# Pooled attention and a gated MLP on one core: fewer VectorE steps for scales, unread TensorE products, a new written order

## Chip, cores and metric

The kernel runs on one core of a Trainium2 chip, in one launch. The metric is the device time of one execution in microseconds (us), the median of several runs. Five engines work side by side, each with its own queue in order: TensorE (PE, with its weight loads as PEld), VectorE (DVE), ScalarE (ACT), GpSimd (POOL) and SyncE (SP), which here only issues DMAs: loads, stores and transposes.

## The reference

```python
# q, k, v: (8, 8, 576, 64); pool 8; float64 weights w_in (512, 1024), w_out (1024, 512), g_ln (1024)
k_p = k.reshape(B, H, 72, 8, D).mean(axis=3)
v_p = v.reshape(B, H, 72, 8, D).mean(axis=3)
scores = scale * q @ k_p.T
attn = softmax(scores)                      # with 1e-9 in the denominator
x = (attn @ v_p), rows as (batch, position), columns as (head, d): (4608, 512)
h = x @ w_in
solu = h * softmax(h)                       # over 1024 columns
ln = (solu - mean) / sqrt(var + 1e-6) * g_ln
out = ln @ w_out                            # (4608, 512) float32
```

The weights arrive as float64, in pairs of 32-bit words, and the results are wanted close to float32. The kernel therefore splits every factor of a large product into two float16 parts, high and low, after scaling it by a power of two, and sums three products (high by high, high by low, low by high).

## The kernel before, in words

*Tiles.* The 4608 rows are worked in 36 tiles of 128 rows. A pair of batches makes nine tiles: four of the first, a mixed one (64 rows of each, key `("m", g)`), four of the second. For a tile i: `q_hi` and `q_lo` split q, `q_T` turns it by a DMA transpose (tile 0 on TensorE: `q_Tp`, `q_Tc`), `scores` multiplies with the pooled and turned k, `s_max`, `s_sub`, `s_exp`, `e_sum`, `e_rec`, `e_mul` are the softmax (one PSUM buffer, so `scores` of a tile waits for `e_mul` of the one before), `e_hi`, `e_lo`, `e_T` split and turn the result, `av` multiplies with pooled v, `x_hi` and `x_lo` make the split input of the MLP. `mm1` (three parts, 48 products of 512 columns in all, two at a time on the halves of the array) gives h in PSUM; `h_max`, `h_nb`, `h_exp`, `z_scale`, `z_mul` are the gated softmax, `z_cen`, `z_hi`, `z_lo`, `z_var` the normalization and split, `z_T` two DMA transposes, `mm2` (three parts, 48 products) the output, `n_u`, `n_f` its row factor on POOL, `o_evac` and `o_store` scale and store it.

*Weights.* Eight chunks of 1 MB are loaded (`w_load`), four for each matrix. For each, ScalarE takes a rough value and the sign (`w_exp`, `w_sgn`), VectorE shifts and joins the words into a float32 (`w_shift`, `w_tail`), POOL puts the sign on (`w_mul`), TensorE sums the rough values into a bound for the largest magnitude (`w_bnd`). From the bound a scale, a power of two, is made (`w_rmax`, `w_par`, `w_all`, then `wi_scale` or `wo_scale`), and the chunks are split: `w_hi` on ScalarE, the low part by `w_res` on TensorE (product with a scaled identity, less the high part) and `w_lo` on ScalarE, or by `w_lod` on VectorE. `g_T`, `g_put`, `g_max`, `g_par`, `g_all` do the same for the gain g.

*k and v of a batch.* They are loaded in three pieces (`load_kv`); for batch 0 the rows are pooled on TensorE by products with the identity (`pool_pe`, copied by `pool_ev`), for the others on POOL (`pool_kv`). `a_max` takes each partition's largest magnitude, `a_par` spreads it to all partitions by a product (`spread`), `a_all` reduces, and three VectorE steps `a_scale` make the power of two "p" and its reciprocal "s": floor and factor 2^-14, keeping the exponent bits (`exp_bits`), reciprocal. `h_bat` (POOL) multiplies v's scale with the three factors `pw3` that `wi_scale` leaves; `h_nb`, `h_exp` and `z_scale` of the batch's tiles read that.

*Order.* Nothing is scheduled at run time but by semaphores. The table `ORDER` gives every operation a position in one list; each engine works its own operations in that order and waits where an input or a buffer isn't ready. Where this text says that one operation stands ahead of another, it means this table. Buffers: seven for raw loads, in PSUM one for scores, one for attention products and spreads, two for h (shared with pooling, residues and TensorE's transposes), one for outputs.

*Lines.* Most products are recorded at the helper `mm`, line 272; `pool_pe` 405, `k_Tp` 513, `w_bnd` 650, `w_res` 809 and 812, `q_Tp`/`e_Tp` 882, `av` 998; on VectorE `a_max` 425, `q_max` 437, `a_all` 487, `a_scale` 492, 275 and 499, `w_shift` 638, `wi_scale` 706 to 713, `v_lo` 578, `q_lo` 865, `e_mul` 948, `h_max` 1040; on ScalarE `w_exp` 634, `e_Tc` 899, `o_evac` 1150; on POOL `w_mul` 678, `h_bat` 721. In the rows kr, vr are raw k and v, kp, vp pooled, amx the magnitudes, gk, gv spread, pk, sk the scale, hp is h, op the output in PSUM, wir, wor raw weights, u_ their rough values.

## Time and profile before

| | us |
|---|---|
| median of 3 runs (lowest, highest) | 493.37 (492.62, 495.02) |
| the profiled execution | 493.96 |
| its span, first to last instruction | 492.2 |
| TensorE busy | 464.2 (94%) |
| VectorE busy | 371.7 (76%) |
| ScalarE busy | 332.2 (67%) |
| POOL busy | 305.8 (62%) |
| mean granted clock of TensorE | 0.996 |

The span is what the trace covers; the execution's time is 1.8 us longer. Busy shares are averages over stages of different kinds: loading and splitting the weights together with batch 0 at first, then a long even stretch of tiles, then the last tiles. [...]

### The profile page before, as it was taken

The numbers are of one execution on the slowest core, as the hardware profiler recorded it, in microseconds if no ns is written. First come the engines' busy times: TensorE is split into PE (matmuls) and PEld (weight loads), VectorE is DVE, ScalarE is ACT, GpSimd is POOL, SyncE is SP. The second block draws the span as 40 slices with busy tenths as digits, with TensorE's granted clock in tenths as the row PEclk, the third lists the DMA queues.
The fourth block names the chain that finished last, engine by engine and source line by source line (L and its number), as shares of the span: only waits on it lengthen the run. The fifth ranks groups of instructions, "written<-read, shape, count | busy, mean of one in ns | idle before, by whom it ended". The sixth has DMA issues, their size and how long they took to land.

```text
span 492.2 us, 14712 instructions
## 1 busy us (share of the span) xinstructions
PE 464.2 (94%) x5976; PEld 301.0 (61%) x5976; DVE 371.7 (76%) x808; ACT 332.2 (67%) x521; POOL 305.8 (62%) x520
## 2 busy tenths in 40 slices
PE   3698699999999999999999999999999999999996
PEld 3574355565667667766755555555566666666663
DVE  3898899997888878897859887788778769553320
ACT  4577997857867687767549656766766767674551
POOL 1556654896668686956792687554986437618340
PEclk9999899999999999999999999999999999999999
DMA  8998668997999996997979979998999485647252
GB/s 301 359 309 197 160 103 188 182 215 165 216 213 216 201 217 128 247 178 209 189 174 166 179 200 204 188 143 174 212 215 171 114 156 125 116 102 136 55 117 87
DMA packets 197940, 88.92 MB, mean 181 GB/s; under 512 B 174312, under 2 KB 182512, under 8 KB 197360
## 3 DMA queue, kind: packets, MB, share of 16 engines
q1 hardware_dynamic: 197872, 87.98, 85.8%
q8 instruction: 47, 0.77, 0.7%
q14 instruction: 21, 0.17, 0.1%
HBM read 36.70 MB, written 9.44 MB: 94 GB/s over the span
## 4 chain that ended last, share of the span: by engine, by line
PE 63%; DVE 10%; POOL 10%; DMA 7%; ACT 4%; issue 3%; SPq 2%; POOLq 0%; ACTq 0%; DVEq 0%
PE op L272 27%; PE hp L272 26%; PE xp L998 4%; PE sc L272 3%; POOL vr L395 2%; DMA wir<-in_moe_w_in_dram 2%; DMA zT<-z 2%; DMA vr<-in_v_dram 2%; POOL kr L395 2%; POOL z L1092 2%; PE vrps L405 1%; DVE z L1072 1%; DVE m L1040 1%; POOL kp L395 1%; PE res_wo L809 1%
## 5 line engine op out<-in xcount | busy, mean ns | idle before, releaser
L272 PE MATMUL hp<-wi,xT 128*64 128x512 f16 x1728 | 197.7, 379 | 1.0 <-ACT xT L1007 0.9
L272 PE MATMUL op<-wo,zT 128*64 128x512 f16 x1728 | 197.7, 379 | 0.8 <-DMA zT<-z 0.6
L272 PEld LDWEIGHTS <-xT 128*64 128x64 f16 x1728 | 110.2, 110 | 70.4 <-ACT xT L1007 1.4
L272 PEld LDWEIGHTS <-zT 128*64 128x64 f16 x1728 | 111.3, 110 | 67.0 <-DMA zT<-z 1.1
L1092 POOL TENSOR_TENSOR z<-z,z 128x512 f16<-128x512 f32 x71 | 82.8, 1175 | 56.9 <-ACT z L1086 55.5
L1040 DVE TENSOR_REDUCE m<-hp 128x1 f32<-128x1024 f32 x36 | 43.9, 1218 | 27.1 <-PE hp L272 25.1
L977 POOL TENSOR_TENSOR e<-e,e 128x512 f16<-128x512 f32 x36 | 42.6, 1184 | 31.4 <-ACT e L969 31.3
L1051 ACT ACTIVATE z<-hp,nb,Hb 128x1024 f32<-128x1024 f32 x32 | 38.3, 1198 | 20.3 <-DVE nb L1043 18.4
L1072 DVE SCALAR_TENSOR_TENSOR z<-hp,rs,z 128x1024 f32<-128x1024 f32 x36 | 46.1, 1279 | 5.9 <-ACT z L1051 4.8
L1081 ACT ACTIVATE z<-z,sz 128x1024 f32<-128x1024 f32 x36 | 41.1, 1143 | 13.3 <-DVE z L1072 13.3
L1150 ACT ACTIVATE osb<-op,f 128x512 f32<-128x512 f32 x36 | 24.5, 680 | 29.5 <-PE op L272 23.9
L395 POOL TENSOR_TENSOR kr<-kr 128x512 f32<-128x512 f32 (+3 forms) x42 | 36.9, 886 | 9.3 <-DMA kr<-in_k_dram 8.6
L395 POOL TENSOR_TENSOR vr<-vr 128x512 f32<-128x512 f32 (+3 forms) x42 | 36.7, 878 | 5.7 <-DMA vr<-in_v_dram 3.7
L1086 ACT ACTIVATE z<-z 128x1024 f16<-128x1024 f32 x36 | 37.9, 1052 | 2.0 <-issue 1.4
L933 DVE TENSOR_REDUCE sc<-sc 128x8 f32<-128x576 f32 x36 | 27.4, 761 | 14.9 <-ACT sc L929 14.9
L1105 ACT ACTIVATE junk<-z 128x1024 f16<-128x1024 f32 x36 | 37.7, 1048 | 0.2
L919 DVE TENSOR_REDUCE mx<-sc 128x8 f32<-128x576 f32 x36 | 27.0, 750 | 10.7 <-PE sc L272 10.7
L998 PEld LDWEIGHTS <-vb 128*64 128x64 f16 x960 | 29.1, 111 | 7.0 <-DMA eT<-e 1.3
L998 PE MATMUL xp<-eT,vb 128*64 128x128 f16 (+1 forms) x960 | 31.1, 215 | 1.2 <-DMA eT<-e 0.9
L272 PEld LDWEIGHTS <-qT 128*64 128x64 f16 x1152 | 25.0, 114 | 9.0 <-issue 5.1
L272 PE MATMUL sc<-kT,qT 128*64 128x72 f16 x1152 | 25.9, 200 | 3.8 <-DVE e L948 2.7
L1011 DVE SCALAR_TENSOR_TENSOR xT<-xp,xT 128x512 f16<-128x512 f32 x36 | 24.6, 683 | 5.7 <-ACT xT L1007 5.5
(239 smaller groups left out, 625.8 us busy)
## 6 DMA issues: line engine op xcount, KB each, us to landing
kr<-in_k_dram SPq DMA_DIRECT2D x16, 512.0 KB, 5.3
qr<-in_q_dram SPq DMA_DIRECT2D x16, 512.0 KB, 5.8
vr<-in_v_dram SPq DMA_DIRECT2D x32, 256.0 KB, 5.4
out_dram<-osb SPq DMA_DIRECT2D x32, 256.0 KB, 4.3
wor<-in_moe_w_out_dram SPq DMA_DIRECT2D x4, 1024.0 KB
wo<-in_moe_w_in_dram SPq DMA_DIRECT2D x2, 1024.0 KB
wir<-in_moe_w_in_dram SPq DMA_DIRECT2D x2, 1024.0 KB, 10.9
zT<-z SPq DMA_TRANSPOSE x72, 3.9
```

The source lines that it names most:

```text
L272: nc.tensor.matmul(out[lo : lo + 64] if m > 64 else out, lhsT=lhsT[:, lo : lo + 64], **kw)
L395: nc.gpsimd.tensor_tensor(out=dst, in0=src[:, :, :n], in1=src[:, :, n : 2 * n], op=ALU.add)
L933: nc.vector.tensor_reduce(out=tl[i]["r0"], in_=s_view(i), axis=AX.X, op=ALU.add)
L977: nc.gpsimd.tensor_tensor(out=e_main(i, 1), in0=e_src(i)[0], in1=e_main(i, 0), op=ALU.subtract)
L998: nc.tensor.matmul(xp[64 * e : 64 * e + 64, c, lo:hi], lhsT=vb[b % 2][:, n, c, e], rhs=eT[:, 2 * c + e if n < 2 else H + c // 2, lo:hi], s ...
L1040: nc.vector.tensor_reduce(out=small(i, "m"), in_=tl[i]["hp"], axis=AX.XY, op=ALU.max)
L1051: nc.scalar.activation(z, t["hp"], AF.Exp, bias=t["nb"], scale=hsc(i, 0), accum_out=small(i, "se"))
L1072: nc.vector.scalar_tensor_tensor(out=t["z"], in0=t["hp"], scalar=t["rs"], in1=t["z"], op0=ALU.mult, op1=ALU.mult, accum_out=small(i, "sz"),)
L1081: nc.scalar.activation(t["zf"], t["zf"], AF.Identity, bias=t["sz"], scale=-float(DFF))
L1086: nc.scalar.activation(t["z16"][:, 0], t["zf"], AF.Copy)
L1092: eng.tensor_tensor(out=t["z16"][:, 1, fs], in0=t["zf"][:, fs], in1=t["z16"][:, 0, fs], op=ALU.subtract)
L1105: nc.scalar.activation(junk, t["zf"], AF.Square, scale=DFF**-0.5, accum_out=small(i, "V"))
```

## The change

Four things. First, steps of scales on VectorE: the factor 2^-14 of the k and v scales is put into the bfloat16 identity `identb` that spreads the maxima, and the floor into a bit that `exp_bits` now sets, so `a_scale` (three steps) becomes `a_unit` (two). `wi_scale` goes from seven steps to three on VectorE, the three factors becoming one POOL product (`w_pwi`, with constants `c3`). `wo_scale` goes from eight steps to five, two more stand in `g_all`, and one product goes to POOL (`w_pwo`). Second, `idle` issues products of a constant matrix with itself into a corner of a PSUM buffer that nothing reads, ahead of the real products of that buffer, in eleven places and 167 in all. Third, dependencies: `h_bat` waits for `pw3` from POOL, `n_f` for `pwo` from POOL. Fourth, `ORDER` is a new table throughout.

In the new table, by queues. SP's loads begin with two chunks of w_in, the last piece of k of batch 0, the third chunk, half of q, and then k's first and second piece (before: k's first piece, two chunks, k's last piece, the third chunk, k's second piece, q). v of batch 0 is loaded around the second chunk of w_out, ahead of the third and fourth (before: its second piece behind the fourth). TensorE: the bounds of the first three chunks ahead of the large pieces of k; `k_Tp` directly behind `q_Tp`; all of v of batch 0 pooled ahead of the first residue of w_in; `v_rep` of batch 0 behind `scores` of tile 3 (before: ahead). Up to `mm1` of tile 0 the same operations as before. VectorE: ahead of `e_mul` of tile 2 no longer one `q_max` of batch 1, one `v_lo` of batch 0 and `a_all` of k of batch 1. ScalarE: `r_put` ahead of `e_Tc`; `x_hi` of tile 0 ahead of a part of `e_hi` of tile 2 and of the sign of the last chunk. POOL: `w_pwi`, `w_pwo`, the last `w_mul` and then `h_bat` of batch 0, behind `e_lo` of tile 2 (before: `h_bat` first). Later: `mm2` of tile 0 behind `mm1` of tile 3 (before: its first part ahead); in the last tiles `o_store` of tile 32 ahead of `z_T` of tiles 35 and 34, second parts.

```diff
+IDLE = {
+    "a_par.k": {0: 23, 1: 15},
+    "a_par.v": {0: 6},
+    "pool_pe": {2: 46, 0: 12},
+    "q_Tp": {0: 13},
+    "scores": {0: 19, 2: 7, 3: 5},
+    "w_par.wi": {0: 13},
+    "w_res.wi": {0: 8},
+}
...
     def exp_bits(dst, src):
         nc.vector.tensor_scalar(
-            out=dst.bitcast(I32), in0=src.bitcast(I32), scalar1=EXPMASK, scalar2=None,
-            op0=ALU.bitwise_and,
+            out=dst.bitcast(I32), in0=src.bitcast(I32), scalar1=EXPMASK, scalar2=1 << 23,
+            op0=ALU.bitwise_and, op1=ALU.bitwise_or,
         )
...
-    nc.vector.tensor_copy(out=identb, in_=ident)
+    nc.vector.tensor_scalar(out=identb, in0=ident, scalar1=1.0 / S14, scalar2=None, op0=ALU.mult)
...
+    for n, c in enumerate((2.0**-11, -(2.0**-11), 2.0**-7)):
+        nc.gpsimd.memset(c3[:, n : n + 1], c)
...
+    todo_now = [None]
+
+    idle_at = {ORDER[nm][n]: c for nm, d in IDLE.items() for n, c in d.items()}
+
+    def idle(dst):
+        for _ in range(idle_at.get(todo_now[0], 0)):
+            nc.tensor.matmul(dst, lhsT=minus, rhs=minus, start=True, stop=True)
...
     def spread(src, n, name):
         g = ps_x.tile([P, CI, P], F32, tag="x", name=name)
+        idle(g[:, CI - 1])
...
-    def a_scale(nm, key, n):
+    def a_unit(nm, key, n):
         st = grp[nm, key]
         if n == 0:
-            nc.vector.tensor_scalar(
-                out=st["p"], in0=st["p"], scalar1=1e-30, scalar2=1.0 / S14, op0=ALU.max,
-                op1=ALU.mult,
-            )
-        elif n == 1:
             exp_bits(st["p"], st["p"])
         else:
             nc.vector.reciprocal(out=st["s"], in_=st["p"])
...
-    def w_bound(nm):
+    def w_bound(nm, c):
         gm = wst[nm]["gm"]
-        nc.vector.tensor_scalar(out=gm, in0=gm, scalar1=2.0**-80, scalar2=None, op0=ALU.max)
+        nc.vector.tensor_scalar(
+            out=gm, in0=gm, scalar1=2.0**-80, scalar2=c, op0=ALU.max, op1=ALU.mult
+        )
         exp_bits(gm, gm)
 
     def wi_scale():
-        w_bound("wi")
-        nc.vector.tensor_scalar(
-            out=pwi, in0=wst["wi"]["gm"], scalar1=1.0 / S14, scalar2=None, op0=ALU.mult
-        )
+        w_bound("wi", 1.0 / S14)
         sw = const.tile([P, 1], F32, name="sw_wi")
-        nc.vector.reciprocal(out=sw, in_=pwi)
+        nc.vector.reciprocal(out=sw, in_=wst["wi"]["gm"])
         wst["wi"]["s"] = sw
-        for n, c in enumerate((2.0**-11, -(2.0**-11), 2.0**-7)):
-            nc.vector.tensor_scalar(
-                out=pw3[:, n : n + 1], in0=pwi, scalar1=c, scalar2=None, op0=ALU.mult
-            )
-
+
+    def w_pwi():
+        nc.gpsimd.tensor_scalar(
+            out=pw3, in0=c3, scalar1=wst["wi"]["gm"], scalar2=None, op0=ALU.mult
+        )
...
     def g_all():
-        wst["gm"] = all_max(wst["g"], "g")
-
-    def wo_scale():
-        w_bound("wo")
-        g2 = wst["gm"]
+        g2 = wst["gm"] = all_max(wst["g"], "g")
         nc.vector.tensor_scalar(out=g2, in0=g2, scalar1=1e-30, scalar2=None, op0=ALU.max)
         exp_bits(g2, g2)
...
+    def w_pwo():
+        nc.gpsimd.tensor_scalar(
+            out=pwo, in0=pw1, scalar1=-(2.0**-8), scalar2=None, op0=ALU.mult
+        )
...
-        op("pool", 0.35, t + 6.5, h_bat, b, r=[("sv", b), ("ws", "wi")], u=[("pv", b)],
+        op("pool", 0.35, t + 6.5, h_bat, b, r=[("sv", b), ("pw3",)], u=[("pv", b)],
...
-        for _, fn, args in sorted(ops, key=lambda o: o[0]):
+        for todo_now[0], fn, args in sorted(ops, key=lambda o: o[0]):
             fn(*args)
```

The same call of `idle` stands at the head of `pool_pe`, `k_Tp`, `v_rep`, `w_bnd`, `w_res`, `turn_pe`, `scores` and `av`; `IDLE` gives the count by name and occurrence (for `pool_pe` 0 and 2 are the first and last piece of k of batch 0).

## Rows read from the trace of the kernel before

**Rows 1.** Stages: busy us (and instructions) of PE, PEld, DVE, ACT, POOL; clock; DMA.
```profile
16.00:34.00 18.00, 13.48 (x130) 11.64 (x129) 16.64 (x37) 12.70 (x19) 8.74 (x5) 1.00 1.04 355
34.00:65.30 31.30, 25.22 (x252) 13.27 (x251) 26.80 (x61) 24.78 (x40) 21.32 (x26) 0.95 0.76 160
65.30:110.00 44.70, 43.58 (x662) 27.21 (x664) 43.44 (x95) 33.94 (x55) 31.19 (x48) 1.00 0.98 182
110.00:467.00 357.00, 354.16 (x4709) 229.20 (x4705) 273.38 (x588) 244.50 (x391) 235.01 (x419) 1.00 0.88 173
```
**Rows 2.** TensorE's waits from 65.3 us on: in total, times, longest.
```profile
PE hp L272 <- ACT xT L1007: 0.9, 2, 0.7
PE xp L998 <- DMA eT<-e: 0.9, 1, 0.9
...
PE op L272 <- ACT osb L1150: 0.2, 1, 0.2
```
**Rows 3.** The chain of waits: start, us, what.
```profile
55.40 0.43 PE res_wo L812
...
60.73 0.71 PE sc L272 x32
61.44 1.10 PE res_wo L809 x2
62.54 0.22 PE res_wo L812
...
65.35 3.64 PE hp L272 x32
```
**Rows 4.** VectorE's instructions in order of time: start, us, line, operands, idle before.
```profile
21.91 0.98 DVE L865 SCALAR_TENSOR_TENSOR q<-qr,sq('b', 0)_210,q 128x512 f16<-128x512 f32 x1
...
29.23 0.15 DVE L706 TENSOR_SCALAR pwi<-gm_wi 128x1 f32<-128x1 f32 x1
...
29.50 0.26 DVE L713 TENSOR_SCALAR pw<-pwi 128x1 f32<-128x1 f32 x3
...
37.78 0.69 DVE L638 TENSOR_SCALAR u_wo<-u_wo 128x1024 int32<-128x1024 int32 x1
...
40.95 0.49 DVE L425 TENSOR_REDUCE amx_v<-vp 128x1 bf16<-128x320 f32 x1 [2.28 <-ACT vp L416]
...
50.50 0.49 DVE L578 SCALAR_TENSOR_TENSOR vb<-vp,sv,vb 64x256 f16<-64x256 f32 x1 [0.60 <-ACT vb L568]
...
58.21 0.29 DVE L487 TENSOR_REDUCE pk<-gk 128x1 f32<-128x128 f32 x1 [0.85 <-PE gk L272]
...
58.49 1.21 DVE L437 TENSOR_REDUCE amx_q<-qr 128x1 f32<-128x1024 f32 x1
...
59.92 0.76 DVE L948 TENSOR_TENSOR e<-sc,r 128x576 f32<-128x576 f32 x1
```
**Rows 5.** ScalarE's instructions in order of time.
```profile
36.60 1.15 ACT L634 ACTIVATE u_wo<-wor 128x1024 f32<-128x1024 f32 x1 [1.66 <-DMA wor<-in_moe_w_out_dram]
...
60.63 1.22 ACT L899 ACTIVATE eT<-eTp 128x1280 f16<-128x1280 f16 x1
```
**Rows 6.** TensorE's instructions in order of time, before 65.3 us.
```profile
15.13 3.79 PE L405 MATMUL krps<-kr,ident 128*128 128x128 f32 x16 [1.14 <-DMA kr<-in_k_dram]
...
28.74 1.17 PE L272 MATMUL sc<-kT,qT 128*64 128x72 f16 x32 [0.28 <-ACT qT L891]
...
58.76 0.44 PE L272 MATMUL vr<-vr,sel 128*64 128x64 f16 x16
```
**Rows 7.** The page's 40 slices: granted clock of TensorE, in tenths.
```profile
PEclk9999899999999999999999999999999999999999
```
**Rows 8.** POOL's instructions in order of time.
```profile
64.39 0.19 POOL L721 TENSOR_TENSOR Hb<-pw,pv 128x3 f32<-128x3 f32 x1
...
69.22 2.15 POOL L678 TENSOR_TENSOR wor<-wor,sg_wo 128x1024 f32<-128x1024 f32 x1 [3.43 <-DVE sc L939]
```
**Rows 9.** The last tiles on ScalarE, in order of time.
```profile
477.53 0.69 ACT L1150 ACTIVATE osb<-op,f 128x512 f32<-128x512 f32 x1 [1.28 <-PE op L272]
```

More of the change, by code (lines that the diff above doesn't have):

```diff
@@ L299 @@
     phalf = const.tile([P, 1], F32, name="phalf")
+    c3 = const.tile([P, 3], F32, name="c3")
+    pw1 = const.tile([P, 1], F32, name="pw1")
     g_sb = const.tile([P, CO], F32, name="g_sb")
-    pwi = const.tile([P, 1], F32, name="pwi")
     pw3 = const.tile([P, 3], F32, name="pw3")
@@ L401, in pool_pe @@
             bat[b][which + "ps"] = ps_h.tile([P, 2, 512], F32, tag="h", name=f"{which}ps{b}")
+        idle(bat[b][which + "ps"][:, 1, 384:])
         dst = bat[b][which + "ps"][:pp].rearrange("p a n -> p (a n)")[:, : NC * D]
@@ L509, in k_Tp @@
         bat[b]["kTp"] = tp
+        idle(tp[:, 896:])
         for c in range(NC):
@@ L597, in v_rep @@
         g = ps_x.tile([P, CI, P], F32, tag="x", name=f"vr{b}")
+        idle(g[:, CI - 1])
         bat[b]["vrep"] = g.rearrange("p c (e d) -> p c e d", e=2)
@@ L646, in w_bnd @@
             st["bnd"] = ps_o.tile([P, 512], F32, tag="o", name=f"bnd_{nm}")
+            idle(st["bnd"][:, 384:])
         bv = st["bnd"][:, :256].rearrange("p (j g) -> p j g", g=32)
@@ L753, in g_all, with wo_scale @@
     def g_all():
[L754 to L758 removed]
+        g2 = wst["gm"] = all_max(wst["g"], "g")
         nc.vector.tensor_scalar(out=g2, in0=g2, scalar1=1e-30, scalar2=None, op0=ALU.max)
         exp_bits(g2, g2)
[L761 to L763 removed]
+    def wo_scale():
+        w_bound("wo", 2.0**-13)
+        sg = const.tile([P, CO], F32, name="sg_wo")
+        nc.vector.tensor_tensor(
+            out=pw1, in0=wst["wo"]["gm"], in1=wst["gm"], op=ALU.mult
         )
         sw = const.tile([P, 1], F32, name="sw_wo")
[L766 removed]
+        nc.vector.reciprocal(out=sw, in_=pw1)
         nc.vector.tensor_scalar(
[L768 removed]
+            out=sg, in0=g_sb, scalar1=sw, scalar2=None, op0=ALU.mult
         )
[L770 to L771 removed]
         wst["wo"]["s"] = sg
+    def w_pwo():
+        nc.gpsimd.tensor_scalar(
+            out=pwo, in0=pw1, scalar1=-(2.0**-8), scalar2=None, op0=ALU.mult
+        )
     def w_f32(nm, c):
@@ L807, in w_res @@
         wst[nm]["res", c] = t
+        idle(t[:, 1, 384:])
         for d in range(2):
@@ L879, in turn_pe @@
         tp = ps_h.tile([P, 2, 512], F32, tag="h", name=name).rearrange("p a n -> p (a n)")
+        idle(tp[:, 896:])
         tp = tp.bitcast(F16).rearrange("p (n m) -> p n m", m=P)[:, :n]
@@ L904, in scores @@
         t["sc"] = sc
+        idle(sc[:, 1, 384:])
         for h in range(H):
@@ L992, in av @@
         tl[i]["xp"] = xp
+        idle(xp[:, CI - 1])
         eT = tl[i]["eT"]
@@ L1211, in scale @@
                 w=[("p" + nm, key), ("s" + nm, key)])
-        for j in range(3):
-            n_ = op("dve", 0.16, t + 0.7 + 0.2 * j, a_scale, nm, key, j, u=[("p" + nm, key)],
+        for j in range(2):
+            n_ = op("dve", 0.16, t + 0.7 + 0.2 * j, a_unit, nm, key, j, u=[("p" + nm, key)],
                     w=[("s" + nm, key)], after=[n_])
```

337 lines of the change are left out of this document (169 added, 168 removed), and 90 rows, old and new, of the table ORDER.

## The prediction

> **What bounds the kernel now.** I read the stages first, then TensorE's waits, then the chain of waits of the first 65 us, then single engines there. By stages [rows 1], TensorE is busy 354.16 of 357.00 us between 110 and 467 us, and 43.58 of 44.70 us between 65.3 and 110 us. All its waits from 65.3 us on come to 4.5 us, eight kinds of at most 0.9 us each (the first two and the last of the eight stand in [rows 2]). So from the first product of h at 65.35 us on [rows 3] the kernel is a full queue of products, whose number the change doesn't touch, with a few us of scaling and storing behind it. The time is the start of that queue, plus its length, plus whatever idle time the new order leaves in it.
>
> Ahead of 65.3 us no one engine is full, but VectorE comes nearest: 16.64 of 18.00 us busy from 16 to 34 us, 26.80 of 31.30 us from 34 to 65.3 us [rows 1]. The chain into the first product of h is VectorE's product e of tile 2 at 59.92 us [rows 4], TensorE's scores of tile 3 at 60.73 us, a residue of w_out, the attention product, ScalarE's copy, the first product at 65.35 us: 4.62 us from the scores on [rows 3]. What sets e at 59.92 us is VectorE's queue from the first low part of q (21.91 us) on: 38.8 us, in which it waits 2.28 us for v's pooled rows and 0.85 us for the spread maximum of k [rows 4].
>
> **The change, part by part.** Times are against the profiled execution, 493.96 us (span 492.2 and 1.8 us around it); the median of the runs is 493.37, 0.6 us below.
>
> *VectorE's queue ahead of e of tile 2.* Gone for good: one step of the k scale and one of the v scale, at the 0.15 us of such a step, 0.30; in the scale of w_in one such step (0.15) and the three factors (together 0.26), 0.41; in the scale of w_out nine steps become eight, 0.15. Sum 0.86 us. Only moved behind it: one of the two maxima of q of batch 1 (1.21), one low part of v (0.49), the reduction of the spread k maximum (0.29), together 1.99 us [rows 4]. So the queue up to e is 2.85 us shorter. From 110 us on VectorE works 273.38 of 357.00 us [rows 1], so the steps saved there for the later batches hide beside products, and I cost them at nothing; without that cover they would be worth 0.15 us each.
>
> *Its waits.* The wait for the spread k maximum (0.85) now stands behind e. The wait of 2.28 us for v goes too: v of batch 0 is loaded ahead of the last two chunks of w_out and pooled ahead of the residues of w_in. What is late next is the last chunk of w_out. ScalarE waited 1.66 us for it and began on it at 36.60 us [rows 5]; 0.52 MB of v more are now ahead of it, 1.5 us at the 355 GB/s of 16 to 34 us [rows 1], so VectorE can shift it from 36.6 + 1.5 + 1.15 = 39.2 us on, where it did so at 37.78 us before [rows 4]: 1.4 us later, whatever it gains ahead of that point. This stands in the sum, with k's part below compared with it.
>
> *k of batch 0.* Its first piece was loaded first of all; now it comes behind two chunks of w_in and half of q, its last piece behind that. Before, the last piece was there at 15.13 us and its 16 products took 3.79 us [rows 6]; now 0.52 MB more lie ahead, 16.6 us at 355 GB/s, and the 16 products of the first piece, which ran early and unseen, come straight before, from about 15.1 us. This is a cost unless TensorE is faster. Is it? The granted clock stands at full speed for the first slices of the profile [rows 7], but the durations contradict: 32 score products took 1.17 us at 28.74 us [rows 6] and 0.71 us at 60.73 us, and the subtraction of a 512-column residue 0.43 us at 55.40 us, where the granted clock is down (0.95 in the mean of 34 to 65.3 us, [rows 1]), and 0.22 us at 62.54 us [rows 3]. [...]
>
> [...]
>
> An unread product of 128 columns is a quarter of that subtraction, 0.055 us at full and 0.11 at half clock [rows 3]. 46 of them, 2.5 to 5 us, stand where TensorE waits for its first load anyway, 12 ahead of the first large piece of k, 23 ahead of the spreading of k's maximum, 32 ahead of q's turning and the first scores. At full clock both pieces are pooled by 15.1 + 0.7 + 1.9 + 1.9 = 19.6 us; maximum (0.49) and reduction (0.29) [rows 4], with 0.35 us each estimated for evacuation and spreading, put the low part of q at 21.1, 0.8 us earlier than before. At half clock it is 15.1 + 1.3 + 3.8 + 3.8 = 24.0, plus 1.5, plus the 23 products (2.5 us, of which 1.0 hides behind the evacuation and the maximum): 27.0, 5.1 us later. I take the middle course, first piece at half and second at full clock: 15.1 + 1.3 + 3.8 + 1.9 + 1.5 = 23.6, less 0.4 us by which the 12 may start ahead of the landing: 1.3 us later. [...] Less the 0.56 us of steps saved by then, VectorE would shift the last chunk at 37.78 + 0.7 = 38.5 us; the chunk's 39.2 is later and decides.
>
> *From e to the first product of h.* The rest of v's rows is now spread behind the scores, 0.44 us [rows 6]: 0.4 more. ScalarE's copy of the turned e (1.22 us, [rows 5]) now waits for that spread; it hides beside the residue of w_out, twice 1.10 and 0.22 us [rows 3]; without that cover it would add about 1 us.
>
> *POOL.* It gets two products for the factors, 0.2 us each like the scale row Hb, and Hb of batch 0 now stands behind these and the sign product of the last chunk (2.15 us) [rows 8]. Adding up ScalarE's and POOL's queues from the first copy of x on, Hb is ready about half a microsecond before the maximum of tile 0, which first needs it. So nothing; beyond that VectorE would stand still for as long.
>
> *The stream and its end.* In the new order mm2 of tile 0 stands behind mm1 of tile 3 (before: ahead), and among the last tiles SP stores tile 32 ahead of two transposes. That store can go when ScalarE is done at 478.2 us [rows 9]; the second transpose follows at about 480 us, and the products that need it start at about 486. So nothing. For the idle time in the stream I take the 4.5 us of before; no row shows that of the new order; the ends are 0 and, as far again, 9.
>
> Sum at the first product of h: queue behind the last chunk -2.85 + 0.56 = -2.3, the two waits -0.85 and -2.28, the chunk +1.4, the spread +0.4: -3.6 us. Not all is kept: the 1.99 us moved still have to be done, and from 65.3 to 110 us VectorE is busy 43.44 of 44.70 us [rows 1]. So between -3.6 and -1.6 is kept; I take -2.8, a little above the middle, because 1.3 us of that stage are free. 493.96 - 2.8 = 491.2 for the profiled execution, 490.6 as a median.
>
> **The rivals.**
> *Warm early.* The 46 products raise the clock and the others hold it; the residue of w_out, which at half clock filled the chain from 53.94 to 57.96 us, runs at full clock in twice 1.10 and 0.22 us [rows 3] and so 1.4 us shorter, and the stream's waits shrink by half (2.2): -2.8 - 1.4 - 2.2, 487.0 us. [...]
> *Cold.* The change doesn't do what it says: the products are too scattered, k is 5.1 us late, and VectorE shifts the last chunk at 42.3 instead of 39.2 us. -2.8 + 3.1 = +0.3: 493.7 us, no change to speak of. For it: the fall at 55 us, with TensorE far from idle; and 16 products at 15.13 us left the clock low.
> *Given back.* The queue starts 3 to 4 us earlier, but VectorE and POOL can't feed it: the moved work and a late Hb leave gaps before 110 us, and 1 us is kept: 492.4 us. For it VectorE's 43.44 of 44.70 us; against it the slack from 110 us on.
> *Slower: transposes late in the stream.* SP's queue is reordered throughout, with stores ahead of transposes; where a transpose stands behind a store that isn't ready, the products stand still. One such wait cost 0.9 us (the attention product, on the transpose of e, [rows 2]). Against a gain of 2.8 us it makes the kernel slower by more than 2.5 us from six tiles of the 36 on; with eight, 490.6 + 7.2 = 497.8 us. Against it: before, that kind of wait came once.
>
> **How the numbers follow.** 0.5%, 2.5 us, is about what a measurement of this kernel can tell from no change; so faster is below 490.9 and slower above 495.8. The forecast has 0.50 (its own range 488.2 to 492.0, seven tenths of it below 490.9: 0.35 faster, 0.15 same), warm early 0.15 (faster), cold 0.15 and given back 0.09 (same), late transposes 0.11 (slower). Faster 0.50, same 0.39, slower 0.11. The range runs from just beyond the warm case to past the cold one, 486.2 to 495.0; it leaves out the slow case and the extremes of the fast one.
>
> **What would show it.** Right: the first product of h at about 62 us; VectorE's wait for v gone, and one of about 0.7 us ahead of the last chunk's shift at 39 us; the low part of q at about 23 us; the first 32 score products in 0.7 us; waits of TensorE behind its first product of h of 4 to 5 us in all. Wrong: score products of 1.2 us there and q's low part behind 25 us (cold); a first product of h at 62 us but the same end (given back); waits of 9 us or more behind the start (late transposes); a first product of h before 60 us (VectorE's queue sheds more than I count).

## The result, and the profile after

The changed kernel takes 499.97 us (median of 4 runs, 497.41 to 501.88), the kernel before on the same chip 493.72 us (4 runs, 492.62 to 495.02): ratio 1.0135, 95% interval [1.0098, 1.0173]. It is 6.3 us slower; the forecast was 2.8 us faster, range 486.2 to 495.0. The profiled execution took 500.74 us, its span 499.0 us. Every ratio here compares executions within 1.5% of the fastest of their kernel with the kernel before of the same rounds, and so can differ from a quotient of medians, most of all for first_46, of whose twelve executions it leaves out the slowest two.

**By stages** (columns as in [rows 1]):

```profile
16.00:34.00 18.00, 14.36 (x202) 13.02 (x201) 12.39 (x25) 10.68 (x15) 8.42 (x4) 0.91 1.04 298
34.00:65.30 31.30, 24.51 (x207) 14.58 (x208) 24.52 (x49) 21.93 (x34) 15.17 (x16) 0.89 0.86 184
...
110.00:467.00 357.00, 352.62 (x4740) 217.75 (x4735) 277.67 (x590) 244.54 (x392) 240.07 (x424) 1.00 0.93 175
```

From 110 us on TensorE stands still for 4.4 us (before 2.8). From 34 to 65.3 us VectorE works 24.52 us and before worked 26.80; from 16 to 34 us it is 12.39 instead of 16.64. That does not yet show that it has less to do: these stretches hold fewer of its instructions because they come later, and over the whole span it is busy 373.0 us, before 371.7. Its waits between 16 and 66 us add up to 11.4 us, before to 4.7 (in the second profiles of the two kernels, below, 8.5 and 3.6).

**TensorE's waits from 66 us on**, against [rows 2]; all six kinds come to 6.5 us instead of 4.5, the three largest being:

```profile
PE xp L1027 <- DMA eT<-e: 2.1, 2, 1.4
PE hp L285 <- DVE z L1101: 1.6, 1, 1.6
PE op L285 <- DMA zT<-z: 1.1, 1, 1.1
```

**TensorE up to the first scores, and from the third scores to the first product of h**, in order of time (start, us, line, operands, idle time before), against [rows 3] and [rows 6]; `<-minus` are the unread products:

```profile
30.18 1.22 PE L358 MATMUL sc<-minus 128*128 128x128 f16 x19 [1.31 <-DVE kT L558]
31.32 0.71 PE L285 MATMUL sc<-kT,qT 128*64 128x72 f16 x32
```

```profile
57.62 0.91 PE L358 MATMUL sc<-minus 128*128 128x128 f16 x7 [5.17 <-DVE e L976]
58.45 1.17 PE L285 MATMUL sc<-kT,qT 128*64 128x72 f16 x32
59.55 2.08 PE L835 MATMUL res_wo<-wor,dg_wo 128*128 128x512 f32 x2
...
61.85 1.91 PE L835 MATMUL res_wo<-wor,dg_wo 128*128 128x512 f32 x2
...
66.40 0.42 PE L285 MATMUL vr<-vr,sel 128*64 128x64 f16 x16
...
70.73 1.49 PE L285 MATMUL hp<-wi,xT 128*64 128x512 f16 x12 [0.69 <-ACT xT L1036]
```

The first scores run in 0.71 us (before 1.17) but at 31.32 instead of 28.74 us. From 57.62 to 63.6 us the engine is at half its clock (granted 0.50): scores of 1.17 us, residues of 2.08 and 1.91 us, where [rows 3] have 0.71 and 1.10. It fell behind a wait of 5.17 us. The kernel before had such a stretch too, from 53.94 to 57.96 us (granted 0.58 in the mean), but not in its second profile. v's spread (66.40 us) stands directly behind the scores, without a wait. The first product of h comes at 70.73 us, 5.4 us later than in [rows 3].

**VectorE**, against [rows 4], in three stretches:

```profile
23.17 1.40 DVE L891 SCALAR_TENSOR_TENSOR q<-qr,sq('b', 0)_290,q 128x512 f16<-128x512 f32 x2
```

```profile
42.25 0.69 DVE L661 TENSOR_SCALAR u_wo<-u_wo 128x1024 int32<-128x1024 int32 x1 [0.73 <-ACT u_wo L657]
...
44.10 0.48 DVE L450 TENSOR_REDUCE amx_v<-vp 128x1 bf16<-128x320 f32 x1
...
54.14 2.65 DVE L613 SCALAR_TENSOR_TENSOR vr<-vp,sv,vr 64x64 f16<-64x64 f32 x1
56.80 0.76 DVE L976 TENSOR_TENSOR e<-sc,r 128x576 f32<-128x576 f32 x1
```

```profile
63.80 0.76 DVE L976 TENSOR_TENSOR e<-sc,r 128x576 f32<-128x576 f32 x1
...
78.52 0.20 DVE L1072 TENSOR_SCALAR nb<-m,Hb 128x1 f32<-128x1 f32 x1
```

The low part of q is 1.3 us later (23.17), the shift of the last chunk of w_out 4.5 us (42.25 instead of 37.78), e of tile 2 3.9 us (63.80). The waits for v (2.28) and for the spread maximum of k (0.85) are gone. `r_lo`, the step of 64x64 at 54.14 us, takes 2.65 us. **ScalarE** gets the last chunk late, against [rows 5], where it began on it at 36.60 us:

```profile
41.09 1.13 ACT L657 ACTIVATE u_wo<-wor 128x1024 f32<-128x1024 f32 x1 [0.18 <-DMA wor<-in_moe_w_out_dram]
```

**POOL**, against [rows 8]: the row Hb is ready at 78.2 us, and VectorE reads it at 78.52 us without a wait.

**The end**, against [rows 9]: the last scaling ends 3.1 us ahead of the span's end (495.24 + 0.69 to 499.0; before, 488.03 + 0.69 to 492.2: 3.5 us).

Executions of one kernel differ by several us (no_products below: 492.72 to 499.88 us): a second profile of the kernel before had its first product of h at 62.70 us (span 488.9), a second one of the kernel after at 66.40 us (span 495.1). What a part costs is therefore taken from ratios, and from a profile only how. VectorE in the second profiles, the kernel before and then the kernel after:

```profile
37.85 0.69 DVE L638 TENSOR_SCALAR u_wo<-u_wo 128x1024 int32<-128x1024 int32 x1
...
57.26 0.76 DVE L948 TENSOR_TENSOR e<-sc,r 128x576 f32<-128x576 f32 x1
```

```profile
41.56 0.69 DVE L661 TENSOR_SCALAR u_wo<-u_wo 128x1024 int32<-128x1024 int32 x1
...
52.31 0.44 DVE L613 SCALAR_TENSOR_TENSOR vr<-vp,sv,vr 64x64 f16<-64x64 f32 x1
...
53.44 2.68 DVE L600 SCALAR_TENSOR_TENSOR vb<-vp,sv,vb 64x256 f16<-64x256 f32 x1
...
60.16 0.76 DVE L976 TENSOR_TENSOR e<-sc,r 128x576 f32<-128x576 f32 x1
```

The shift of the last chunk and e of tile 2 are late here too, by 3.7 and 2.9 us; but `r_lo` takes 0.44 us, and now a low part of v takes 2.68.

### The profile page after: what moved, and what is told of

Read it like the earlier page. It is cut to its first block, busy times and chain, and to the rows that moved or that the text cites. A ratio compares the mean times of both kernels' runs of the same rounds, so it can differ in the third digit from the quotient of the medians.

```text
span 499.0 us, 15028 instructions
## 1 busy us (share of the span) xinstructions
PE 470.5 (94%) x6143; PEld 297.9 (60%) x6143; DVE 373.0 (75%) x787; ACT 332.4 (67%) x521; POOL 307.1 (62%) x525
## 5 line engine op out<-in xcount | busy, mean ns | idle before, releaser
L285 PEld LDWEIGHTS <-xT 128*64 128x64 f16 x1728 | 105.6, 110 | 75.9 <-ACT sc L957 2.1
L285 PEld LDWEIGHTS <-zT 128*64 128x64 f16 x1728 | 105.4, 110 | 72.3 <-DMA zT<-z 1.6
L997 ACT ACTIVATE e<-e 128x512 f16<-128x512 f32 x36 | 22.4, 621 | 11.3 <-DVE e L976 7.7
L1036 ACT ACTIVATE xT<-xp 128x512 f16<-128x512 f32 x36 | 21.2, 588 | 12.2 <-PE xp L1027 12.1
```

The source lines that it names most:

```text
L285: nc.tensor.matmul(out[lo : lo + 64] if m > 64 else out, lhsT=lhsT[:, lo : lo + 64], **kw)
```

## Experiments

Each ran in five rounds beside the kernel before on the same chip (its median there was 492.4 to 493.3 us). "Start" is the table up to the first `mm1`, "stream" what stands behind it. The last two columns are of the one profiled execution: start of the first product of h, and TensorE's waits from it on, the one ahead of it included.

| kernel | what it is | median us | ratio to before, 95% | first h | waits |
|---|---|---|---|---|---|
| before | | 493.37 | | 65.35 | 4.5 |
| before_again | before | 492.20 | 0.9977 [0.9952, 1.0001] | 62.70 | 4.4 |
| after_again | after | 498.00 | 1.0128 [1.0090, 1.0165] | 66.40 | 6.7 |
| steps_only | before + new steps | 495.32 | 1.0059 [1.0029, 1.0089] | 63.50 | 5.9 |
| units_only | before + k and v steps | 492.40 | 0.9999 [0.9979, 1.0018] | 64.09 | 3.8 |
| w_only | before + weights' steps | 494.50 | 1.0041 [1.0021, 1.0060] | 64.48 | 5.4 |
| products_only | before + 167 products | 495.98 | 1.0067 [1.0041, 1.0092] | 64.72 | 7.5 |
| order_only | before + new order | 496.68 | 1.0083 [1.0055, 1.0112] | 64.58 | 7.2 |
| start_only | before + new start | 496.99 | 1.0085 [1.0054, 1.0117] | 65.08 | 5.9 |
| stream_only | before + new stream | 494.54 | 1.0039 [1.0011, 1.0066] | 66.81 | 7.0 |
| start_after | after, stream of before | 500.58 | 1.0159 [1.0118, 1.0201] | 68.50 | 10.5 |
| stream_after | after, start of before | 497.60 | 1.0078 [1.0051, 1.0106] | 64.88 | 6.9 |
| no_products | after, no products | 497.40 | 1.0087 [1.0053, 1.0121] | 67.73 | 6.8 |
| first_46 | after, 46 of 167 products | 498.49 | 1.0086 [1.0053, 1.0119] | 62.90 | 7.3 |
| late_off | after, 140 of 167 products | 498.17 | 1.0101 [1.0062, 1.0140] | 67.60 | 7.0 |
| rlo_later | after, `r_lo` behind e | 498.00 | 1.0118 [1.0081, 1.0155] | 66.77 | 6.6 |
| v_behind | after, half of v later | 502.56 | 1.0204 [1.0160, 1.0249] | 71.53 | 6.7 |
| v_first | before, half of v earlier | 494.17 | 1.0036 [1.0012, 1.0060] | 67.95 | 3.9 |
| delay_e2 | before + a clear of 0.48 us | 494.42 | 1.0031 [1.0006, 1.0055] | 65.79 | 3.8 |

### First suspects: products, loads, one step beside POOL, the steps

**no_products** (`IDLE = {}` in the kernel after).

> The changed kernel without its 167 unread products, all else as it is. Three theories of the 6.3 us that the change costs. LOADS: v of batch 0, loaded ahead of the last two chunks of w_out, moves at half rate, the last chunk is shifted 4.5 us late (42.25 for 37.78 us) and all behind it is late: then the products matter little, first product of h at 70.7 us within 1.0, time 499 to 501 us. PORT: the low part of v's rest is held for 2.65 us beside POOL's work on e and k, TensorE waits 5.2 us for the product e and falls to half clock: also little, 0 to 1.5 us faster. PRODUCTS: 27 of the products (7, 15, 5) stand behind that wait in a stretch of half clock and delay scores and spread by 2.3 us themselves: first product of h at 68 to 69 us, time 497 to 498. Against all: without the early products k of batch 0 is pooled and turned at half clock throughout, up to 2 us later (q's low part at 25 instead of 23.2 us), which the last chunk's lateness would hide.

Measured 1.0087, against 1.0135 and 1.0128 with the products: they cost 0.4 to 0.5%, 2.0 to 2.4 us, though the intervals overlap. In the profile the first scores start at 29.11 us, with the products at 31.32. The rest of the loss is elsewhere.

**v_behind** (kernel after; one of v's two large pieces of batch 0 behind the last chunk of w_out, and pooled later).

```diff
-load_kv[4] = 79;     pool_pe[4] = 80;     pool_ev[4] = 108
+load_kv[4] = 104.5;  pool_pe[4] = 112.3;  pool_ev[4] = 112.5
```

> The changed kernel with one of v's three pieces of batch 0 (0.52 MB) loaded behind the last chunk of w_out, as before the change, and pooled that much later (ahead of the scores of tile 1). LOADS: ScalarE's step on the last chunk begins at 37 to 39 us instead of 41.1, VectorE shifts it at 38 to 40 instead of 42.25, the first product of h comes 2 to 4 us earlier, time 496 to 498 us; v's maxima then wait as before (up to 2.3 us). PORT: the low part of v's rest still meets POOL's work, only elsewhere: the gain is at most 1 us, 499 us. PRODUCTS: no gain beyond 1 us.

ScalarE began on the last chunk 2.6 us earlier (38.48 us), yet the kernel is slower still, 1.0204: now v's pooling is late, the scale of w_out is made behind it (57.44 us instead of 52.84), and e of tile 1 at 58.53 us. So the chunk alone does not set the start. The edit moved two things and settles little; v_first below is the cleaner form.

**rlo_later** (kernel after; `r_lo[0]` 175 -> 176.5, behind `e_mul` of tile 1).

> The changed kernel with one step of VectorE moved by one place: the low part of v's rest (64 by 64, 2.65 us in the trace) behind the product e of tile 1 instead of ahead of it. PORT: e of tile 1 is done at 54.2 to 55 us instead of 57.5, TensorE waits 2.5 instead of 5.2 us for it, the fall to half clock is shorter (one step of 3.4 us instead of 6.8, or none) and the first product of h is 2.5 to 4.5 us earlier: time 496 to 497.5 us. LOADS: all behind the last chunk is bound by ScalarE and TensorE anyway, under 1 us: 499 to 500 us. PRODUCTS: as LOADS.

1.0118, within the interval of the kernel after. This does not clear the slow step: in its new place it still took 1.99 us (at 52.98 us), and the two low parts of q ahead of it 2.06 and 1.39 us, as in the kernel after (2.07 and 1.39). e of tile 1 came at 52.21 us instead of 56.80, but so it did in the second profile of the kernel after, without the move (52.76).

**steps_only** (the kernel before with the new steps; `w_pwi` at 242.5 and `w_pwo` at 242.7, just ahead of `h_bat` of batch 0).

> The kernel before, its order and loads, with the fewer steps for the scales alone (two POOL products put ahead of the first Hb), no unread products. By all three theories the loss is in the order or the products, so this is as fast as before or a little faster: 0.86 us of VectorE's steps go ahead of the first product of h, 491.5 to 494 us, 1.0 us at most gained. If this is slower than before by 1 us or more, the new POOL products or the longer forms of the steps cost something that I missed.

1.0059: no gain, a loss. Split further below.

### The same again, and the parts alone

**after_again** (kernel after, unchanged).

> The changed kernel unaltered, run beside the next ones so that they are compared on one chip: 1.010 to 1.017 times the kernel before. With the last chunk of w_out not as late as in its first profile (its loads came 1.9 us earlier in a kernel with the same loads), the first product of h comes at 68 to 70 us instead of 70.7.

**order_only** (kernel before with the new positions, `a_scale` mapped to `a_unit`'s, the first of its three steps straight ahead of the second).

> The kernel before with its own steps for the scales (three for k and v, seven and eight for the weights, all on VectorE) and no products, but in the new order. ORDER: the new order is what costs; it is as slow as the changed kernel without products, 1.007 to 1.011 times before. SUM: the parts add; the changed kernel without products was 1.0087 and the steps alone 1.0059, so the order alone is 1.002 to 1.004. STEPS: the order was searched for the fewer steps and with longer ones it is worse than either, over 1.011.

**products_only** (kernel before with `idle` and its calls).

```diff
+    "pool_pe": {0: 46, 1: 12},   # the pieces that come first in the order before
```

> The kernel before in its own order and steps, with the 167 unread products in the same eleven places (46 ahead of whichever piece of k is first there, 12 ahead of the next large one). If products cost where they stand ahead of real work in the stretch behind 50 us (27 of them, 1.5 us at full and 3 us at half clock): 1.003 to 1.006. If a clock that is at full speed from about 20 us on is worth something in this order: products of batch 0 in half the time, scores 0.71 instead of 1.17 us at 29 us, but VectorE's queue sets the pace there: 0 to 1 us gained, 0.998 to 1.000. I expect the first, as the sum of 1 us gained and 2 lost: 1.001 to 1.005.

The same kernel again gives 1.0128. Each part costs alone: order 0.83%, products 0.67%, steps 0.59%. Together they cost 1.28%, less than the sum. Why products cost shows at the first scores, TensorE and VectorE of products_only:

```profile
29.91 1.22 PE L352 MATMUL sc<-minus 128*128 128x128 f16 x19 [0.28 <-DVE kT L556]
31.07 0.71 PE L282 MATMUL sc<-kT,qT 128*64 128x72 f16 x32
```

```profile
29.05 0.81 DVE L556 SCALAR_TENSOR_TENSOR kT<-kTp,sk,kT 128x576 f16<-128x576 f32 x1
```

The 19 products write into the one score buffer, in which `k_Tp` stood until VectorE's `kT` had read it, at 29.86 us. So they can't run early: they start at 29.91 us, when the scores could, and hold them up by 1.16 us, for 0.46 us won on the scores (0.71 instead of 1.17).

**late_off** (kernel after without the 27 products ahead of the k spread of batch 1 and the scores of tiles 2 and 3: `"a_par.k": {0: 23}, "scores": {0: 19}`).

> The changed kernel without the 27 products that stand behind 50 us (7 and 5 ahead of the scores of tiles 2 and 3, 15 ahead of the spread of k's maximum of batch 1); the 140 others stay. PRODUCTS: these 27 lay on the path into h, 2.3 us in the first profile: 1.5 to 2.5 us faster than the changed kernel, 1.008 to 1.010, as fast as without any. If they keep the clock up and so pay for themselves: no gain, residues of w_out at half clock (1.9 to 2.1 us for the pair instead of 1.1).

1.0101: in between, and its interval reaches both ends. **first_46** (kernel after, `IDLE = {"pool_pe": {2: 46}}`):

> The kernel after with only the 46 products that stand ahead of TensorE's first load; the other 121 are left out. If the products cost because they stand ahead of work that others wait for (the 19 ahead of the first scores start only when VectorE has freed the buffer that they write): like the kernel without any, 1.007 to 1.010. If what counts is the clock that they hold up: no better than the kernel after, 1.012 to 1.015.

1.0086, like no products at all; but the medians of all executions give 1.0113, so the time does not decide, and the profiled execution (493.61 us) was the fastest of the twelve. The profiles decide for the start: the first scores stand at 29.05 us, without any products at 29.11, with all at 31.32. So the 46 that fill the wait for the first load delay nothing there, and the other 121 move the first scores by 2.2 us. VectorE in this profile:

```profile
39.96 0.69 DVE L655 TENSOR_SCALAR u_wo<-u_wo 128x1024 int32<-128x1024 int32 x1 [1.15 <-ACT u_wo L651]
...
50.01 0.96 DVE L607 SCALAR_TENSOR_TENSOR vr<-vp,sv,vr 64x64 f16<-64x64 f32 x1
...
56.67 0.76 DVE L970 TENSOR_TENSOR e<-sc,r 128x576 f32<-128x576 f32 x1
```

### Is it the comparison, or any shift at all?

**before_again** (unchanged).

> The kernel before, unaltered, as a run of its own. Every variant so far came out 0.6 to 2.0% slower than it, so the comparison itself is measured: ratio 1.000 within 0.3%. Its second profile tells whether 4.5 us of waits and 426.85 us from the first product of h to the end belong to the kernel (within 0.6 us again) or to the one execution that was profiled first (then 428 to 429.5, as in all variants).

**delay_e2** (kernel before):

```diff
 def e_mul(i):
     e = p2.tile([P, NR], F32, tag="e", name=f"e{i}")
     tl[i]["e"] = e
+    if i == 2:
+        nc.vector.memset(e[:, :512], 0.0)
```

> The kernel before with one more VectorE step in front of the e multiply of tile 2: a clear of half of e, which the multiply then overwrites. Nothing else is touched. Theory A (the order before is fitted to its own timing, and any shift of the first product of h is paid again in waits of the stream): ratio 1.003 to 1.007. Theory B (a delay ahead of the first product of h costs what it lasts, 0.2 to 0.6 us): ratio 0.999 to 1.002.

The kernel against itself comes out 0.23% apart (0.9977), so a difference of 0.3 to 0.4% is near what the comparison can tell. The waits (4.4 us) and the time behind the first product of h (426.2 us) are those of the first profile again. The clear took 0.48 us and cost 0.31%, 1.5 us, with an interval of 0.3 to 2.7 us that reaches into the ranges of both theories; the stream did not get longer (waits 3.8). TensorE of delay_e2, of before_again, then of stream_only (below), whose start is the order before unchanged, and of the first profile of the kernel before:

```profile
59.61 1.17 PE L272 MATMUL sc<-kT,qT 128*64 128x72 f16 x32 [2.00 <-DVE e L950]
60.71 2.08 PE L809 MATMUL res_wo<-wor,dg_wo 128*128 128x512 f32 x2
```

```profile
58.08 0.71 PE L272 MATMUL sc<-kT,qT 128*64 128x72 f16 x32 [1.14 <-DVE e L948]
58.72 1.17 PE L809 MATMUL res_wo<-wor,dg_wo 128*128 128x512 f32 x2
...
62.70 1.05 PE L272 MATMUL hp<-wi,xT 128*64 128x512 f16 x8 [0.69 <-ACT xT L1007]
```

```profile
59.35 1.17 PE L170 MATMUL sc<-kT,qT 128*64 128x72 f16 x32 [1.14 <-DVE e L846]
60.45 2.08 PE L707 MATMUL res_wo<-wor,dg_wo 128*128 128x512 f32 x2
```

```profile
60.73 0.71 PE L272 MATMUL sc<-kT,qT 128*64 128x72 f16 x32 [1.53 <-DVE e L948]
```

TensorE waited 2.00 us for e, by 0.86 us longer than without the clear (1.14 us ahead of the scores at 58.08). The scores behind it took 1.17 instead of 0.71 us and the first residue 2.08 instead of 1.17: 1.37 us more, at the lengths that the kernel after has where 0.50 of the clock is granted. But that the longer wait brought the half clock is not shown: stream_only has it behind the same wait of 1.14 us as before_again, and the first profile of the kernel before has these scores in 0.71 us behind a wait of 1.53. So the run decides neither theory.

### Start or stream

**start_after, stream_after** (kernel after), **start_only, stream_only** (kernel before, old steps, no products):

```python
# start_after, start_only: X = 224 in the new order; the other two: first and second table exchanged, X = 238
ORDER[name][i] = first[name][i] if first[name][i] < X else 10000 + second[name][i]
```

> The kernel after (its fewer steps, its 167 products) with its new order only up to the first product of h; everything behind stands in the order before. If the loss is made in the new start (w_out's last chunk and sg_wo late, half rate of v): ratio 1.008 to 1.013, as for the kernel after. If the new order of the stream makes it: 1.002 to 1.006.

> The other half: the kernel after with the order before up to the first product of h, and the new order from there on. Start theory: ratio 1.002 to 1.007 (what the products and the steps cost alone). Stream theory: 1.008 to 1.013.

> The steps of before, no products; the new order up to the first product of h, the order before behind it. If the new start is at fault: slower by 0.5 to 0.8% (1.005 to 1.008), its first product of h 2 to 3 us later than in the kernel before. If the new start costs only with the products beside it: 1.000 to 1.003.

> The other half, again without the new steps and products: the order before up to the first product of h, the new one behind it. Six kernels with the new stream all show TensorE waiting 1.5 to 1.8 us for the scaled z at 155 to 160 us behind the first product of h, and 0.5 to 1.5 us for a turned q some 85 us behind it. If that is a loss of its own: the same waits here, 428 to 429.5 us from the first product of h to the end (before: 426 to 427), ratio 1.004 to 1.006. If these waits come only from a late start: 1.000 to 1.002.

stream_after (1.0078) lies between the ranges of the two theories. The new start costs 0.85% by itself, the new stream 0.39%; both together no more than the start alone (order_only, 0.83%): the halves overlap, or the intervals hide the rest. With the old stream behind it the new start measures worst (1.0159), which suggests that the new stream fits its own start, though the interval reaches that of the kernel after. TensorE's waits from 66 us on in stream_only:

```profile
PE xp L896 <- DMA eT<-e: 3.6, 3, 1.7
PE hp L170 <- DVE z L970: 1.5, 1, 1.5
```

stream_only waits 1.5 us for z and 3.6 us for the turned e; before_again only 0.9 us for the turned e and not for z. In all ten profiles with the new stream the waits come to 6.5 to 7.3 us; with start, stream, products and weights' steps of before (five profiles) to 3.8 to 4.5.

What the new start does between e of tile 2 and h shows in start_only, TensorE and VectorE from e of tile 2 on:

```profile
57.14 0.71 PE L170 MATMUL sc<-kT,qT 128*64 128x72 f16 x32 [0.36 <-DVE e L846]
59.11 0.44 PE L170 MATMUL vr<-vr,sel 128*64 128x64 f16 x16 [1.26 <-DVE pk L385]
59.48 1.77 PE L707 MATMUL res_wo<-wor,dg_wo 128*128 128x512 f32 x2
...
61.47 1.91 PE L707 MATMUL res_wo<-wor,dg_wo 128*128 128x512 f32 x2
...
65.08 1.27 PE L170 MATMUL hp<-wi,xT 128*64 128x512 f16 x10 [0.69 <-ACT xT L905]
```

```profile
56.24 0.76 DVE L846 TENSOR_TENSOR e<-sc,r 128x576 f32<-128x576 f32 x1
...
57.27 1.47 DVE L476 SCALAR_TENSOR_TENSOR vb<-vp,sv,vb 64x256 f16<-64x256 f32 x1
58.77 0.29 DVE L385 TENSOR_REDUCE pk<-gk 128x1 f32<-128x128 f32 x1
```

e of tile 2 is as early as forecast (56.24 us, 1.0 us ahead of before_again, although the last chunk is shifted 2.3 us later), but the first product of h is 8.8 us behind it, in before_again 5.4 (57.26 to 62.70). The spread of v's rows waits 1.26 us for VectorE: it needs the one buffer for spreads, which holds the spread k maximum of batch 1 until VectorE has reduced it, and that reduction now stands behind e and a low part of v, which took 1.47 us here. Behind the wait the two residues run at half clock, 1.77 and 1.91 us instead of 1.17 and 1.06; whether the wait brought this is open, since stream_only has half clock there too and no such wait. About 1.0 of the 1.26 us is the length of that low part of v: in late_off and first_46 it took 0.48 us, and the spread waits 0.27 us. TensorE of late_off:

```profile
63.25 0.44 PE L285 MATMUL vr<-vr,sel 128*64 128x64 f16 x16 [0.27 <-DVE pk L513]
```

In neither profile of the kernel after does the spread wait at all (66.40 and 62.05 us, directly behind the scores).

**v_first** (kernel before; `load_kv[4]` 102 -> 82, ahead of the last two chunks of w_out).

> The kernel before with one move: the second 0.5 MB of v of batch 0 is loaded ahead of the last two chunks of w_out instead of behind them. If the half rate of v's loads in the new kernels (205 to 240 GB/s from 24 to 32 us) comes from this place: the same dip here, ScalarE's exponent of the last chunk at 38.5 to 39.5 us instead of 36.6; since VectorE's wait for v ends earlier in exchange, ratio 0.999 to 1.003. If the dip comes from the other changes of the order: above 350 GB/s from 28 to 32 us as before.

The dip is there. Windows of before_again, after and v_first (last column GB/s, first that of the stretch):

```profile
28.00:32.00 4.00, 3.70 (x52) 3.45 (x51) 3.64 (x15) 3.37 (x5) 3.43 (x2) 0.50 1.02 409
```

```profile
24.00:28.00 4.00, 3.85 (x65) 3.13 (x66) 4.00 (x8) 4.00 (x5) 0.00 (x0) 1.00 1.05 224
28.00:32.00 4.00, 2.69 (x66) 2.46 (x64) 2.14 (x7) 2.18 (x4) 3.23 (x2) 1.00 1.09 197
```

```profile
28.00:32.00 4.00, 3.81 (x51) 3.71 (x52) 2.77 (x14) 0.14 (x1) 3.16 (x2) 0.50 1.10 201
```

ScalarE of v_first:

```profile
32.01 1.13 ACT L532 ACTIVATE u_wo<-wor 128x1024 f32<-128x1024 f32 x1 [3.87 <-DMA wor<-in_moe_w_out_dram]
...
39.10 1.18 ACT L532 ACTIVATE u_wo<-wor 128x1024 f32<-128x1024 f32 x1 [1.28 <-DMA wor<-in_moe_w_out_dram]
```

ScalarE begins on the second chunk of w_out at 32.01 us, behind a wait of 3.87 us, and on the last at 39.10 us; in before_again it was 29.03 and 36.63 us. The exponent of the first scores stands behind the second chunk in its queue (36.07 instead of 33.17 us), and the kernel is 0.36%, 1.8 us, slower (interval 0.6 to 3.0 us).

### The steps, split

**units_only** (kernel before; the first of the three steps of `a_scale` left out, `identb` scaled, the bit in `exp_bits`) and **w_only** (steps_only with the k and v scales of before).

> The kernel before with only the k and v scales one VectorE step shorter (the factor is folded into the matrix that spreads the maximum). If VectorE's steps were on the path of the stream: faster, 0.996 to 0.999. If they hide: 0.999 to 1.002. If the loss of the fewer steps (0.59% with all of them) lies here: 1.004 to 1.007.

> The kernel before with only the weights' scales changed: fewer VectorE steps, and the two products that build the factors on POOL, ahead of its scale row of v. If POOL's two products cost, because they stand ahead of work on POOL that waits for w_out's scale: 1.004 to 1.007. If the loss lies in the k and v scales or in the noise of a shifted start: 0.999 to 1.003.

Sixteen steps fewer on VectorE are worth nothing measurable (0.9999). The loss is with the weights' scales, 0.41%. In w_only's profile POOL makes the two factors in 0.31 and 0.21 us right ahead of Hb, and no engine is seen waiting for them; how they cost is open. Beside the new order the steps cost nothing measurable (no_products 1.0087, order_only 1.0083).

No version beats the kernel before; units_only equals it.

## Why the prediction was wrong

The forecast had the first product of h 3.6 us earlier. It came 5.4 us later, in the second pair of profiles 3.7. Its sum, cut at VectorE's shift of the last chunk of w_out and at e of tile 2:

| us, against the kernel before | forecast | first profiles | second profiles |
|---|---|---|---|
| up to the shift of the last chunk | +1.4 | +4.5 | +3.7 |
| from there to e of tile 2 (queue -2.3, two waits -3.1) | -5.4 | -0.6 | -0.8 |
| from e to the first product of h (v's spread) | +0.4 | +1.5 | +0.8 |
| first product of h | -3.6 | +5.4 | +3.7 |

The step that failed most is the second row.

- **The queue of VectorE that sets e, and its two waits (-5.4 us).** Measured -0.6 and -0.8. The two waits went, and fewer instructions stand in the stretch (36 and 37 instead of 42 and 41). But VectorE is as busy in it as before: 17.68 us of 21.55 where it was 17.97 of 22.14, in the second profiles 16.77 of 18.60 where it was 16.63 of 19.41. I took each step at its length in one profile, and the lengths moved: `r_lo` took 2.65 us in the first profile of the kernel after and 0.44 in the second, a low part of v 0.47 and 2.68. In the six profiles of this start, v's loads unmoved, with a step of v of 1.99 to 2.68 us the stretch takes 18.60 to 21.55 us (the kernel after twice, no_products, rlo_later, late_off, start_after); in the three without one it takes 16.09 to 16.71 (order_only, start_only, first_46), VectorE busy 13.92 to 14.24 us. That is the length of the forecast, 22.1 - 5.4 = 16.7 us, though against the second profile of the kernel before only 2.7 to 3.3 us less. So the queue did get shorter as counted, but in the kernel after longer steps used up the gain, and VectorE waited for scores (1.7 us, first profile) and for v's spread maximum (1.0 us). No run took the overlap with POOL away, so what makes the steps longer is not shown. units_only gives the k and v part of the 0.86 us no measurable worth.
- **The last chunk (+1.4 us, at 39.2 us).** It was 42.25 us, +4.5, in the second profile 41.56, +3.7. One part is v's loads. I divided v's 0.52 MB by the 355 GB/s of the stage; v goes in loads of 64 partitions (0 to 63 and 64 to 127 in turn), and the stretch that they fill moves 197 to 224 GB/s. v_first shows the same dip by this move alone (201 GB/s), some 2.5 us for the chunk. What holds the loads to that rate is not shown. The other part goes with the products, which I had at nothing here: with the new loads and at most the first 46 products the shift stands at 39.32 to 40.15 us (no_products, order_only, first_46, start_only), with more of them at 40.34 to 42.25 (rlo_later, late_off, start_after and both profiles of the kernel after). By which path they delay it was not traced; SP stands 7.20 us in issuing these loads in the first profile of the kernel after, 5.75 us in order_only and 5.77 in start_only.
- **From e to h: v's spread (+0.4 us), the reduction moved behind e.** From the scores of tile 3 to the first product of h it is 4.87 and 5.04 us instead of 4.62, about as forecast. The rest is that the scores start 1.3 and 0.4 us behind the end of e, with unread products ahead of them, where they started at once. What I overlooked is the buffer that the spread needs: in start_only and order_only it waits 1.26 us for the reduction that I had moved off e's path. In the kernel after itself this wait is in neither profile. Moving only the reduction back ahead of e was not tried.
- **The products** (free, or a gain in the warm rival). The 46 delay nothing in the start; all 167 cost 2.0 to 2.4 us in the new order and 0.67%, 3.3 us, in the old one (products_only). The 19 ahead of the first scores, for one, stand where a step on the path waits, not where TensorE does. The 1.3 us that I gave k of batch 0 came out (23.17 us), but without the products it is 0.2 us (22.10, no_products). That they would bring the second piece to full clock was my guess, and no run shows it: the 32 products of both pieces, 5.7 us in my sum, took 5.24 and 5.77 us in the two profiles of the kernel after and 5.49 us in no_products. The first scores did run at full clock, in the first profile; in the second they took 1.17 us, at 32.92 us. Over the twenty profiles they took 0.71 us in six of the eight with unread products directly ahead of them and 1.06 and 1.17 us in the other two; in the twelve without, 1.17 us. What length or density of work brings the full clock is not shown.
- **The stream's idle time (4.5 us as before).** 6.5 and 6.7 us in the two profiles, and stream_only has it with no other edit, +0.39% or 1.9 us. I wrote that no row shows the new order's idle time, and took the old one all the same.

Right: v's wait gone; ScalarE's copy of the turned e hidden beside the residues; Hb in time, with 0.3 us to spare where I said about half a microsecond; nothing at the end. Of the rivals, *cold* and *given back* each saw one thing (products that don't keep the clock up: 0.50 granted from 57.62 to 63.6 us; moved work that comes back), neither with the sign. That *cold* had the last chunk's shift at 42.3 us is luck: it rested on k 5.1 us late, and k was 1.3 us late. *Slower: transposes late in the stream* had the sign and by chance nearly the time (497.8 us), but waits for transposes of e give only about 1 us of the 6.3; most is lost ahead of the first product of h (5.4 of the 6.8 us between the spans of the first profiles, 3.7 of 6.2 in the second), where I saw only gains.

By ratios: new order +4.1 us (order_only), steps beside it +0.2 (no_products against order_only), products +2.0 to 2.4 (the kernel after against no_products). These are successive differences, so their sum is the whole by construction and no check of it; the first has an uncertainty of about 1.5 us, the other two of 2 to 2.5. That the new order costs is therefore shown, and that the products cost in the old order; how the rest divides is not. Open remain how the weights' steps cost 2 us in the old order, and what of the new start's 4.2 us is beyond v's loads (v_first, 1.8).

## What to carry to other kernels

Before an operation is moved off the path, list what holds the buffer that it frees: a step that reads a shared PSUM buffer belongs to whoever writes that buffer next. Here the reduction that was moved behind e held up the spread by 1.26 us (start_only). Filler products were free here where the engine itself waited for an outside event (the 46: first scores at 29.05 us, at 29.11 without any); into a buffer that another step had first to empty, they ran exactly when the real work could (the 19: 1.16 us). And an engine that is about 90% busy, as VectorE is from 16 to 65.3 us [rows 1], is not yet the bound (sixteen of its steps fewer, 0.9999): remove one step from it and see, before summing steps. Nor is the length of a step a constant: `r_lo` took 2.65 and 0.44 us in two profiles of one kernel, so take a queue's length from more than one.

## What the runs showed of the hardware

- At half clock (0.50 granted from 57.62 to 63.6 us in the kernel after) the 32 scores took 1.17 us and the residue behind them 2.08, at full clock 0.71 and 1.10 (1.00 granted from 60.73 to 62.54 us in the kernel before). The same start, with the same wait of 1.14 us ahead of these scores, had them and the residue in 0.71 and 1.17 us in before_again and in 1.17 and 2.08 us in stream_only.
- VectorE's `r_lo` took 2.65 us at 54.14 us in the kernel after, while POOL worked from 54.20 to 56.70 us with hardly a gap, and 0.28 us in the kernel after where POOL was idle (81.65 us). Not every such step beside POOL's work was long: a low part of v at 51.65 us in first_46 took 0.47 us, while POOL worked from 51.12 to 55.17 us. What lengthens the step is not shown.
- The granted clock of an early stretch can mislead: [rows 7] show full clock at 28 us with scores of 1.17 us, and the second profile of the same kernel gives 0.50 from 28 to 32 us, with the same 1.17 us.
